# Attention with a fused gated feed-forward: down-projection matmuls cut into smaller pieces, buffers tracked by halves, and the last outputs finished in halves

## The chip, the cores and the metric

The kernel runs on one core of a Trainium2 chip. Five engines work on their own queues: TensorE (PE; its weight loads are shown as PEld), VectorE (DVE), ScalarE (ACT), GpSimd (POOL) and SyncE (SP), which here only issues DMAs. The metric is device time in microseconds of one launch; lower is better.

## The reference

`x` has 2048 rows and 448 columns. The core of the computation is:

```
xn = layernorm(x)
q  = (xn @ wq) as 16 heads of 256;  k, v = last 512 rows of the caches, 8 heads, each used by 2 query heads
s  = softmax(q k^T / 16) v, heads side by side, @ wo            # wo: 4096 x 448
g  = silu((gelu(xn @ w_gate) * (xn @ w_up)) @ w_down)           # 448 -> 1792 -> 448
out = x + s * g
```

The kernel folds `wo` into the values: for each head, V Wo (512 x 448) is computed once, and then P V Wo takes the place of P V and the output projection.

## The kernel before

The whole instruction order is written out by hand. `K.op` records an operation with the buffers that it reads and writes; a planner turns them into semaphore waits. Two records that name the same buffer object are ordered, even if they touch different halves of it. Each engine executes its own operations in the order of recording, so an operation that waits holds up all that is behind it on its engine. Every matmul is recorded by `mms` (L384 in the profile), every ScalarE operation with a plain function by `act` (L378).

**Stage 1** (to about 119 us): layer norm, gate and up projections; V Wo of heads 0 and 1 and the down tiles 0 to 7 (a down tile is 128 rows of `g`, 14 matmuls of 448 columns) are done in it.

**Stage 2, V Wo** (119 to 158 us): the loop over `order`. It alternates half a down tile (7 matmuls, PSUM bank 4 or 5) with `vw_head`: 8 matmuls of one head into four banks of the ring 0, 1, 2, 3, 6, 7. Down tiles 8 to 13 are done here. Heads 13, 14 and 15 come last with nothing between them, and heads 14 and 15 both use banks 0 to 3. `vw_mm` empties a bank: for row blocks 0 and 1 ScalarE writes part 0 (L713) and VectorE part 4 from the bank and part 0 (L715); for blocks 2 and 3 ScalarE writes parts 1 and 2 (L719). `vw_sums` (L726, VectorE) then forms the parts 5, 6 and 3. The seven parts are the right-hand sides of a seven-product (Strassen-Winograd) scheme for P V. Each part holds two row blocks, jj = 0 and 1, and is one buffer `b_vw[h][part]`.

A finished down tile goes through `down_gate`: ScalarE Tanh, VectorE product (L581), and a DMA of the gate to DRAM, issued by `store_g`.

**Stage 3**: the first queries, then 128 steps; step n is head n % 16 of the 256-row chunk n // 16. `halves` issues matmuls on the two 64-row halves of TensorE side by side. In step n TensorE computes the scores of step n (`s_jobs`, two tiles in the banks 4, 5, 6 in rotation), the queries of step n + 2 (`q_jobs`; bank 7, and in the first four steps bank 1 for the second half of the columns), and P V of step m = n - 4 (`pv_plan`, seven products into banks 0 to 3, which add up over the 16 heads of a chunk). VectorE takes the reciprocal of the last step's row sums (`rd`, L863), two row minima (L852) and the four sums of P blocks of step n - 3 (`sums`, L888); ScalarE copies the queries out of PSUM (`q_evac`) and takes two exponentials (`expo`, L857); GpSimd normalises P (L873) and SyncE transposes it with a DMA. The order on VectorE and ScalarE is that of these lines:

```
            row_min(n, 0)
            if more:
                q_evac(n + 2)
            ...
            row_min(n, 1)
            expo(n, 0)
            expo(n, 1)
            if 3 <= n < NST - 1:
                sums(n - 3, (0, 1, 2))
                if ends:
                    evac(1, "dve")
                sums(n - 3, (3,))
```

In the steps 0 to 3 there is no P V. `fill(0)` before the steps and `fill(1)` to `fill(3)` after the steps 0 to 2 do the last two down tiles, 14 and 15, in halves of 7 matmuls.

**Chunk ends.** At steps n = 19, 35, ... 115 (`ends`) a chunk's seven sums are copied out of the banks 0 to 3: `evac(0)` and `evac(1)` on VectorE, `evac(2)` and `evac(3)` on ScalarE. `finish` makes a list of small operations (adds on GpSimd, products with the gate on VectorE), and each following step pops one from `todo`. For most chunks these are 13 operations on 224 columns; for the last chunk but one (c = 6, finished in chunk 7's steps) they are 8 operations on up to 448 columns.

**The end.** The last four heads (P V of steps 124 to 127) are done as plain products after the loop. For this `vw_plain` (L1045, VectorE) forms a further sum for the heads 12 to 15, in the steps 123 to 126, and `gates_scaled` (ScalarE) scales the last two gates, in the steps 120 and 123.

Of the kernel before, what the change touches and what calls it, by code (L numbers as in the profile page):

```python
# [166 lines left out]
def bass_recurrent_scan__sliding_block_cached__geglu_ffn__prompt_kernel(  # L167
# [36 lines left out]
    with es:  # L204
# [80 lines left out]
        vw, a, _ = place("vw", [P, Hq, 7, 2, HN], F16, at=rv)  # L285
        b_vw = [[K.buf(a + vslot(h) * VWB + p * 2 * HN * 2, 2 * HN * 2) for p in range(7)] for h in range(Hq)]
        aS, a, at = place("aS", [P, 7, HN], F32, at=tl)
# [80 lines left out]
        x_view = A_x.rearrange("b (t p) d -> p (b t) d", p=P)  # L368
        out_view = out.rearrange("b (t p) d -> p (b t) d", p=P)

        def dma(q, o, i, reads=(), writes=()):
# [335 lines left out]
        def vw_mm(h, j, i):  # L707
            o, b = bank[i][:, 0:D], b_ps[i]
            mms([(o, vT_at(h // 2)[:, e, j * P:(j + 1) * P], wo_at(2 * h + e), e == 0, e == 1) for e in range(2)],
                [b_vT[h // 2], b_wo[h]], (b,))  # L710
            v, jj = vw[:, vslot(h), :, :, :], j % 2
            if j < 2:
                K.op("act", lambda e: e.activation(v[:, 0, jj, :], o[:, 0:HN], ACT.Copy, scale=sc[:, 0:1]),  # L713
                     (b, b_sc), (b_vw[h][0],))
                K.op("dve", lambda e: e.scalar_tensor_tensor(  # L715
                    out=v[:, 4, jj, :], in0=o[:, HN:D], scalar=sc[:, 0:1], in1=v[:, 0, jj, :],
                    op0=ALU.mult, op1=ALU.subtract), (b, b_sc, b_vw[h][0]), (b_vw[h][4],))
            else:
                K.op("act", lambda e: e.activation(  # L719
                    v[:, 1:3, jj, :], o.rearrange("p (a n) -> p a n", a=2), ACT.Copy, scale=sc[:, 0:1]),  # L720
                    (b, b_sc), b_vw[h][1:3])

        def vw_sums(h):
            v = vw[:, vslot(h), :, :, :]
            for o, a, b in ((5, 2, 4), (6, 5, 0), (3, 1, 5)):
                K.op("dve", lambda e, o=o, a=a, b=b: e.tensor_tensor(v[:, o, :, :], v[:, a, :, :], v[:, b, :, :], ALU.subtract),  # L726
                     (b_vw[h][a], b_vw[h][b]), (b_vw[h][o],))

        def vw_head(h, banks, last=True):
            K.reuse(b_vw[h])  # L730
# [94 lines left out]
        def q_evac(n):  # L825
            s, i = n % NQT, bq(n)
            if 2 <= n < 2 + LAG:
                for e, i in ((0, 7), (1, 1)):
                    act(qT[:, s, e, :], bank[i][:, e * CW:(e + 1) * CW], ACT.Copy, (b_ps[i],), b_qT[s][e:e + 1], scale=NEG)
            else:  # L830
                act(qT[:, s, :, :].rearrange("p e q -> p (e q)"), bank[i], ACT.Copy, (b_ps[i],), b_qT[s], scale=NEG)
# [46 lines left out]
        def sums(n, parts):  # L878
# [7 lines left out]
            for p in parts:  # L886
# [6 lines left out]
                          ((4, 0), (4, 1), (5, 0), (5, 1)), ((3, 0), (3, 1)))  # L893
        FIRST = {(0, (1, 0)), (0, (4, 0)), (0, (3, 0)), (1, (6, 0))}
        LAST = {(1, (2, 1)), (0, (7, 1)), (1, (5, 1)), (1, (3, 1))}
# [8 lines left out]
        def pv_jobs(n, u, lst, last):  # L904
            h, src = n % Hq, pv_src(n)
            rows = slice(R * u, R * u + R)
            out = []
            for p, j in lst:
                i, s = AT[p]
                a, b = src[p]  # L910
                out.append([i, s * HN, (s + 1) * HN, a[rows, j, :], vw[rows, vslot(h), p - 1, j, :],
                            h == 0 and (u, (p, j)) in FIRST, (u, (p, j)) in last, [b, b_vw[h][p - 1]]])
            return out

        def pv_plan(n):
            if n % Hq == Hq - 1:
                one, mid, two, all_ = B0 + B2 + B1[:1], B3, B1[1:], B0 + B1 + B2 + B3
            elif n % Hq == 0:
                one, mid, two, all_ = B0 + B2, (), B3 + B1, B0[:2] + B1 + B0[2:] + B2 + B3
            else:  # L920
                one, mid, two, all_ = B0 + B2, (), B1 + B3, B1 + B3 + B2 + B0
            last = LAST if n % Hq == Hq - 1 else TLAST if n == NST - LAG - 1 else ()
            u = 0 if n + LAG + 2 < NST else 1
            return [pv_jobs(n, u, x, last) for x in (one, mid, two)] + [pv_jobs(n, 1 - u, all_, last)]

        def flat(x):
            return [z for y in x for z in y]

# [27 lines left out]
        def finish(c, eng):  # L956
# [32 lines left out]
            a1, a0, a6 = tt([1], [0], [1]), tt([0], [2], [5]), tt([6], [0], [6])  # L989
            if c == NC - 2:  # L990
                z = (0, 1)
                return [a1, a0, tt([4, 5], [3], [4, 5]), fin(1, z), a6, add(1, z), fin(0, z), add(0, z)]
            u, v = (0,), (1,)
            return [a1, a0, tt([4], [3], [4]), fin(1, u), tt([5], [3], [5]), fin(1, v), add(1, u), fin(0, u), a6,
                    add(1, v), fin(0, v), add(0, u), add(0, v)]

        heads = [*range(3, 13), 2, 13]
        order = []
        for i, h in enumerate(heads):
            order += [8 + i / 2, h]  # L1000
        order += [14, 15]
        ring = [0]

        def banks4():
            r = [(0, 1, 2, 3, 6, 7)[(ring[0] + i) % 6] for i in range(4)]
            ring[0] += 4
            return r

        for k in order:
            if isinstance(k, float):  # L1010
                t, f = int(k), 0 if k == int(k) else NF // 2
                i = 4 + t % 2
                down_mm(t, bank[i][:, 0:D], [b_ps[i]], f, f + NF // 2)
                if f:
                    down_gate(t, bank[i][:, 0:D], [b_ps[i]])
                    store_g()
            elif k < 14:
                vw_head(k, banks4())
                if k in (8, 10):
                    y = k // 10  # L1020
                    K.reuse(b_xq[y])
                    load_xq(y)
            else:
                vw_head(k, (0, 1, 2, 3))
        js = [[q_jobs(n, e) for e in range(2)] for n in range(2)]
# [7 lines left out]

        def fill(k):
            t, i, f = NT - 2 + k // 2, (0, 2)[k // 2], k % 2 * NF // 2
            down_mm(t, bank[i][:, 0:D], [b_ps[i]], f, f + NF // 2)
            if f:
                down_gate(t, bank[i][:, 0:D], [b_ps[i]])
        K.reuse(b_p32 + flat(b_pn) + b_pT[:3] + flat(b_sS[:2]) + b_tmpr + b_g2r)

        VW12 = {NST - LAG - 1 + i: Hq - LAG + i for i in range(LAG)}

        def vw_plain(h):
            v = vw[:, vslot(h), :, :, :]
            K.op("dve", lambda e: e.tensor_tensor(v[:, 6, :, :], v[:, 4, :, :], v[:, 0, :, :], ALU.add),  # L1045
                 (b_vw[h][4], b_vw[h][0]), (b_vw[h][6],))

# [3 lines left out]
        b_gsl = sbuf_bufs(a, D * 4, 2)  # L1051
        GS = {NST - 8: 0, NST - 5: 1}

        def gates_scaled(t):
# [4 lines left out]
        todo, stores, ready = [], [], []  # L1059
        fill(0)  # L1060
        for n in range(NST):
            h, m = n % Hq, n - LAG
            c = n // Hq
            more = n + 2 < NST
            ends = m >= 0 and m % Hq == Hq - 1
            if n == LAG:
                store_g()
                K.reuse(b_pT[3:] + b_sS[2])
            s0, s1 = s_jobs(n, 0, True), s_jobs(n, 1, not more)
            for t in ready:  # L1070
# [4 lines left out]
            if more:  # L1075
                q0, q1 = q_jobs(n + 2, 0), q_jobs(n + 2, 1)
                q0[1][0][5] = True
                (q1[0] if m >= 0 else q1[1])[-1][6] = True
                if m < 0:
                    q1[0][0][5] = q0[0][-1][6] = True  # L1080
            if m < 0:
                halves(q1[0] + s0[0] + q0[0] + s1[0], q0[1] + s1[1] + q1[1] + s0[1])
            else:
# [17 lines left out]
            if 3 <= n < NST - 1:  # L1101
                sums(n - 3, (0, 1, 2))
                if ends:
                    evac(1, "dve")
                sums(n - 3, (3,))
            if n < 3:
                fill(n + 1)
            if n == 2:
                store_g()
            if n in VW12:  # L1110
                vw_plain(VW12[n])
            if n in GS:
                gates_scaled(GS[n])
            if n == LAG:
# [3 lines left out]
            if ends:  # L1118
                evac(3, "act")
                todo.extend(finish(m // Hq, "pool"))  # L1120
            elif todo:
                todo.pop(0)()
            if h == LAG and c >= 1 and c + 1 < NC:
# [51 lines left out]
        for n, t in [(n, t) for n in range(NST - LAG, NST - 2) for t in range(2)] + [  # L1175
# [6 lines left out]
                  n == NST - LAG and j == 0, n == NST - 1 and j == 3) for j in range(4)],  # L1182
                [b_late[t] if n == NST - 1 else b_pT[x]] + [b_vw[h][k] for k in (0, 1, 2, 6)], [b_ps[i]])
        for t in range(2):
# [62 lines left out]
```

## Time and profile before

| | |
|---|---|
| time, median of 3 runs (lowest to highest) | 556.69 us (556.63 to 556.80) |
| the profiled execution's own time | 556.68 us |
| its span, first to last instruction | 554.9 us |
| granted TensorE clock, mean | 1.000 |
| busy: PE, PEld, DVE, ACT, POOL | 98%, 79%, 84%, 62%, 45% of the span |
| stage 2 with the first queries and the first half tile | 119.1 to 161.7 us |
| steps 0 to 4 | 161.7 to 177.2 us |

A line of the timeline gives the start and the length in us, the engine, the line of the kernel, the operation, what it writes and reads, how many instructions were merged, and in brackets how long the engine stood idle before and what ended the wait. A busy TensorE is not TensorE at its best rate: matmuls are pipelined and their ends are modelled, so a small delay can show as a longer distance between starts and not as idle time.

### The profile page before, as it was taken

To read this page: it belongs to the slowest core of one execution; us is meant where nothing else is said; L and a number is where in the kernel's file an instruction comes from. 1 tells how busy PE (TensorE), PEld (TensorE's weight loads), DVE (VectorE), ACT (ScalarE), POOL (GpSimd) and SP (SyncE) were. 2 spreads that over 40 slices of the span, in tenths; PEclk is the share of its full clock that TensorE was granted. 3 is DMA by queue.
4 is the path that set the end of the run, shared out by engine and by line. 5 is a ranking of instruction groups with operands and counts; after the bars stand their busy time and mean duration, and the time that the engine had idled before them with its cause. 6 is when DMAs were issued, how large, how long until landed. Compare 5 with 4: busy or idle time off the path is not lost.

```text
span 554.9 us, 18732 instructions
## 1 busy us (share of the span) xinstructions
PE 544.7 (98%) x7612; PEld 437.6 (79%) x7612; DVE 465.5 (84%) x1196; ACT 341.3 (62%) x813; POOL 250.3 (45%) x385
## 2 busy tenths in 40 slices
PE   8999999999989999999999999999999999999996
PEld 5544444445546999999999999999999999999983
DVE  6674979867757888988988898898989889889996
ACT  5432323477766676776766676676676666666762
POOL 1121590100004444566465465555556555564655
PEclk9999999999999999999999999999999999999999
DMA  9998999401105866566675775576686477566665
GB/s 274 178 242 146 226 270 216 103 1 41 41 8 97 132 108 97 96 98 105 128 107 102 128 108 93 117 125 107 91 135 107 89 128 118 94 108 125 89 106 81
DMA packets 190246, 66.07 MB, mean 119 GB/s; under 512 B 169408, under 2 KB 187984, under 8 KB 190160
## 3 DMA queue, kind: packets, MB, share of 16 engines
q1 hardware_dynamic: 186928, 56.96, 59.6%
q0 software_dynamic: 2464, 7.34, 4.5%
q8 instruction: 60, 0.98, 0.7%
q10 hardware_dynamic: 768, 0.57, 0.3%
q14 instruction: 26, 0.21, 0.2%
HBM read 19.76 MB, written 5.77 MB: 46 GB/s over the span
## 4 chain that ended last, share of the span: by engine, by line
PE 86%; DVE 9%; DMA 2%; issue 1%; ACT 1%; POOL 0%; SPq 0%; DVEq 0%; ACTq 0%
PE bank L384 86%; DVE mn L852 1%; DVE sS L888 1%; DVE vw L715 1%; DVE vw L726 1%; DVE actT L559 1%; DMA x<-in_A_x_dram 1%; DMA pT<-pn 1%; ACT vw L713 1%; DVE mx L676 1%; DVE xn L457 0%; DVE stats L431 0%; ACT gl L378 0%; DVE g2a L581 0%; POOL rstd L443 0%
## 5 line engine op out<-in xcount | busy, mean ns | idle before, releaser
L384 PE MATMUL bank<-kT,qT 64*128 64x512 bf16 x1024 | 279.1, 376 | 0.0
L873 POOL TENSOR_SCALAR pn<-p,rd 128x512 f16<-128x512 f32 x254 | 173.1, 695 | 227.6 <-DVE rd L863 227.6
L384 PE MATMUL bank<-vw,sS 64*128 64x224 f16 x1984 | 222.3, 256 | 0.8 <-DVE sS L888 0.5
L384 PE MATMUL bank<-xq,wq 64*128 64x256 bf16 x1536 | 218.5, 269 | 0.1
L384 PE MATMUL bank<-vw,pT 64*128 64x224 f16 (+1 forms) x1520 | 208.7, 258 | 0.8 <-DMA pT<-pn 0.8
L852 DVE TENSOR_REDUCE mn<-bank 128x1 f32<-128x512 f32 x256 | 173.9, 683 | 35.3 <-PE bank L384 32.5
L857 ACT ACTIVATE p<-bank,mn 128x512 f32<-128x512 f32 x256 | 175.1, 685 | 5.4 <-PE bank L384 3.2
L384 PEld LDWEIGHTS bank<-vw,sS 64*128 64x128 f16 x1984 | 160.7, 94 | 7.8 <-DVE sS L888 2.5
L378 ACT ACTIVATE qT<-bank 128x512 bf16<-128x512 f32 (+1 forms) x132 | 76.6, 584 | 116.6 <-PE bank L384 115.5
L384 PEld LDWEIGHTS bank<-vw,pT 64*128 64x128 f16 (+1 forms) x1520 | 142.5, 94 | 6.1 <-DMA pT<-pn 1.5
L384 PEld LDWEIGHTS bank<-xq,wq 64*128 64x128 bf16 x1536 | 139.6, 94 | 9.4 <-issue 1.9
L384 PEld LDWEIGHTS bank<-kT,qT 64*128 64x128 bf16 x1024 | 93.5, 94 | 2.1 <-ACT p L857 1.2
L888 DVE TENSOR_TENSOR sS<-pT 128x256 f16<-128x256 f16 x248 | 89.8, 402 | 0.0
L384 PE MATMUL bank<-xnT,wgu 64*128 64x512 bf16 (+2 forms) x768 | 84.5, 350 | 0.8 <-DVE actT L559 0.3
L384 PE MATMUL bank<-xq,wqr 64*128 64x256 bf16 x256 | 67.5, 269 | 0.0
L384 PEld LDWEIGHTS bank<-xnT,wgu 64*128 64x128 bf16 x768 | 36.6, 94 | 38.3 <-DVE actT L559 1.1
L378 ACT ACTIVATE gl<-bank 128x512 bf16<-128x512 f32 x56 | 33.1, 597 | 48.5 <-PE bank L384 40.1
L857 ACT ACTIVATION_READ_ACCUMULATOR p<-bank,mn 128x1 f32 x256 | 50.7, 198 | 0.0
L559 DVE TENSOR_TENSOR actT<-bank,gl 128x512 bf16<-128x512 f32 x56 | 37.4, 686 | 15.5 <-PE bank L384 14.8
L384 PE MATMUL bank<-wd,actT 128*128 128x448 bf16 x224 | 45.4, 353 | 0.6 <-DVE actT L559 0.5
L888 DVE TENSOR_TENSOR sS<-pT,sS 128x256 f16<-128x256 f16 x124 | 36.1, 291 | 4.0
L384 PEld LDWEIGHTS bank<-wd,actT 128*128 128x128 bf16 x224 | 21.3, 98 | 22.7 <-issue 1.7
(83 smaller groups left out, 418.5 us busy)
## 6 DMA issues: line engine op xcount, KB each, us to landing
wq<-in_A_wq_dram POOLq DMA_DIRECT2D x8, 384.0 KB, 9.7
woa<-in_A_wo_dram POOLq DMA_DIRECT2D x6, 448.0 KB, 5.3
pT<-pn SPq DMA_TRANSPOSE x129, 3.1
xn_t<-xnT SPq DMA_DIRECT2D x16, 128.0 KB, 3.6
xr<-in_A_x_dram SPq DMA_DIRECT2D x16, 112.0 KB, 2.6
gr<-gate_t SPq DMA_DIRECT2D x16, 112.0 KB, 2.7
out_dram<-ofin SPq DMA_DIRECT2D x16, 112.0 KB, 2.0
wd<-in_B_w_down_dram SPq DMA_DIRECT2D x1, 1568.0 KB, 8.1
```

The costliest lines, as they stand in the source:

```text
L378: K.op("act", lambda e, o=o, i=i: e.activation(o, i, func, scale=scale), reads, writes)
L384: ins = e.matmul(o, lhsT=l, rhs=r, start=st, stop=sp)
L559: K.op("dve", lambda e: e.tensor_tensor(actT[c % 2][:, f, :], bank[b + 1], gl[:, s, :], ALU.mult), (b_ps[b + 1], b_gl[s]), (b_actT[c % 2][ ...
L676: K.op("dve", lambda e: e.tensor_reduce(mx[:, i:i + 1], o, AX.XY, ALU.max, apply_absolute_value=True), (b,), (b_mx,))
L713: K.op("act", lambda e: e.activation(v[:, 0, jj, :], o[:, 0:HN], ACT.Copy, scale=sc[:, 0:1]), (b, b_sc), (b_vw[h][0],))
L715: K.op("dve", lambda e: e.scalar_tensor_tensor(out=v[:, 4, jj, :], in0=o[:, HN:D], scalar=sc[:, 0:1], in1=v[:, 0, jj, :], op0=ALU.mult, op ...
L726: K.op("dve", lambda e, o=o, a=a, b=b: e.tensor_tensor(v[:, o, :, :], v[:, a, :, :], v[:, b, :, :], ALU.subtract), (b_vw[h][a], b_vw[h][b] ...
L852: K.op("dve", lambda e: e.tensor_reduce(mn[:, m:m + 1], bank[i], AX.X, ALU.min), (b_ps[i],), (b_mn[m],))
L857: K.op("act", lambda e: e.activation(p32[:, z, :], bank[i], ACT.Exp, bias=mn[:, m:m + 1], scale=-1.0, accum_out=rsum[:, 2 * r + t:2 * r + ...
L873: K.op(engs[t], lambda e, o=o, i=i, s=s: e.tensor_scalar(o, i, s, 1.0, op0=ALU.mult, op1=ALU.mult), (b_p32[z], b_rd[r]), (b_pn[y][t],))
L888: o = K.op("dve", lambda e, i=i, a=a, b=b, f=f: e.tensor_tensor(s[i], a, b, f), r, (b_sS[y][i],))
```

## The change

Seven things are changed.

1. `b_vw` has a buffer for each half (jj = 0, 1) of each part. Every user of it names the halves it touches.
2. The down tiles 8 to 15 (112 matmuls) are cut into 19 pieces by `down_piece(n)`, which goes on where the last piece ended, across tiles: 6 or 7 matmuls before each of the first twelve heads, 6 before head 14, 4 before head 15, 4 before the first step, and 5 after each of the steps 0 to 3. Tile 14 uses bank 0 as before, tile 15 bank 3 (bank 2 before). Head 14 uses the banks 1, 2, 3, 6, and head 15 7, 1, 2, 3.
3. In the first four steps the second half of the queries is copied out of bank 1 by VectorE, between the two row minima; the first half stays on ScalarE. The matmuls of these steps begin with the scores in one half and with the queries in the other.
4. At a chunk end `evac(1)` stands after the first two sums, not after the first three, and the first P V of a chunk takes part 7 before part 6 in bank 1.
5. The first finishing operation is popped in the chunk-end step itself.
6. The last chunk but one is finished in 13 small operations like the others; at steps 120 and 124 two are popped.
7. `vw_plain` of the heads 12 and 13 moves from the steps 123 and 124 to 113 and 114, and both `gates_scaled` to step 126.

The diff, cut to its core:

```diff
-        b_vw = [[K.buf(a + vslot(h) * VWB + p * 2 * HN * 2, 2 * HN * 2) for p in range(7)] for h in range(Hq)]
+        b_vw = [[sbuf_bufs(a + vslot(h) * VWB + p * 2 * HN * 2, HN * 2, 2) for p in range(7)] for h in range(Hq)]
...
                 K.op("act", lambda e: e.activation(v[:, 0, jj, :], o[:, 0:HN], ACT.Copy, scale=sc[:, 0:1]),
-                     (b, b_sc), (b_vw[h][0],))
+                     (b, b_sc), (b_vw[h][0][jj],))
...
-                for e, i in ((0, 7), (1, 1)):
-                    act(qT[:, s, e, :], bank[i][:, e * CW:(e + 1) * CW], ACT.Copy, (b_ps[i],), b_qT[s][e:e + 1], scale=NEG)
+                act(qT[:, s, 0, :], bank[7][:, 0:CW], ACT.Copy, (b_ps[7],), b_qT[s][0:1], scale=NEG)
+                K.op("dve", lambda e: e.tensor_scalar(qT[:, s, 1, :], bank[1][:, CW:2 * CW], NEG, None, op0=ALU.mult),
+                     (b_ps[1],), b_qT[s][1:2])
...
-        FIRST = {(0, (1, 0)), (0, (4, 0)), (0, (3, 0)), (1, (6, 0))}
+        FIRST = {(0, (1, 0)), (0, (4, 0)), (0, (3, 0)), (1, (7, 0))}
...
-                one, mid, two, all_ = B0 + B2, (), B3 + B1, B0[:2] + B1 + B0[2:] + B2 + B3
+                one, mid, two, all_ = B0 + B2, (), B3 + B1, B0[:2] + B1[2:] + B1[:2] + B0[2:] + B2 + B3
...
-            if c == NC - 2:
-                z = (0, 1)
-                return [a1, a0, tt([4, 5], [3], [4, 5]), fin(1, z), a6, add(1, z), fin(0, z), add(0, z)]
...
+        down_at = [NT // 2 * NF]
+        def down_piece(n):
+            while n:
+                t, f = divmod(down_at[0], NF)
+                k = min(n, NF - f)
+                i = 4 + t % 2 if t < NT - 2 else (0, 3)[t - NT + 2]
+                down_mm(t, bank[i][:, 0:D], [b_ps[i]], f, f + k)
+                down_at[0] += k
+                n -= k
+                if f + k == NF:
+                    down_gate(t, bank[i][:, 0:D], [b_ps[i]])
+                    if t < NT - 2:
+                        store_g()
         heads = [*range(3, 13), 2, 13]
+        ring = (0, 1, 2, 3, 6, 7)
         for i, h in enumerate(heads):
-            order += [8 + i / 2, h]
-        order += [14, 15]
+            down_piece(6 + (i in (0, 3, 5, 8, 10, 11)))
+            vw_head(h, [ring[(4 * i + j) % 6] for j in range(4)])
...
+        down_piece(6)
+        vw_head(14, (1, 2, 3, 6))
+        down_piece(4)
+        vw_head(15, (7, 1, 2, 3))
...
-        VW12 = {NST - LAG - 1 + i: Hq - LAG + i for i in range(LAG)}
+        VW12 = {NST - Hq + 1: 12, NST - Hq + 2: 13, NST - 3: 14, NST - 2: 15}
...
-        GS = {NST - 8: 0, NST - 5: 1}
...
-        fill(0)
+        down_piece(4)
         for n in range(NST):
...
-                halves(q1[0] + s0[0] + q0[0] + s1[0], q0[1] + s1[1] + q1[1] + s0[1])
+                halves(s0[0] + s1[0] + q0[0] + q1[0], q0[1] + q1[1] + s0[1] + s1[1])
...
-                sums(n - 3, (0, 1, 2))
+                sums(n - 3, (0, 1))
                 if ends:
                     evac(1, "dve")
-                sums(n - 3, (3,))
-            if n < 3:
-                fill(n + 1)
+                sums(n - 3, (2, 3))
+            if n < LAG:
+                down_piece(5)
...
-            if n in GS:
-                gates_scaled(GS[n])
+            if n == NST - 2:
+                gates_scaled(0)
+                gates_scaled(1)
...
                 todo.extend(finish(m // Hq, "pool"))
-            elif todo:
-                todo.pop(0)()
+            for _ in range(2 if n - NST + Hq in (8, 12) else 1):
+                if todo:
+                    todo.pop(0)()
```

More of the change, by code (lines that the diff above doesn't have):

```diff
@@ L369, in bass_recurrent_scan__sliding_block_cached__geglu_ffn__prompt_kernel, with flat @@
         out_view = out.rearrange("b (t p) d -> p (b t) d", p=P)
+        def flat(x):
+            return [z for y in x for z in y]
         def dma(q, o, i, reads=(), writes=()):
@@ L713, in vw_mm @@
                 K.op("act", lambda e: e.activation(v[:, 0, jj, :], o[:, 0:HN], ACT.Copy, scale=sc[:, 0:1]),
-                     (b, b_sc), (b_vw[h][0],))
+                     (b, b_sc), (b_vw[h][0][jj],))
                 K.op("dve", lambda e: e.scalar_tensor_tensor(
                     out=v[:, 4, jj, :], in0=o[:, HN:D], scalar=sc[:, 0:1], in1=v[:, 0, jj, :],
-                    op0=ALU.mult, op1=ALU.subtract), (b, b_sc, b_vw[h][0]), (b_vw[h][4],))
+                    op0=ALU.mult, op1=ALU.subtract), (b, b_sc, b_vw[h][0][jj]), (b_vw[h][4][jj],))
             else:
@@ L720, in vw_mm @@
                     v[:, 1:3, jj, :], o.rearrange("p (a n) -> p a n", a=2), ACT.Copy, scale=sc[:, 0:1]),
-                    (b, b_sc), b_vw[h][1:3])
+                    (b, b_sc), (b_vw[h][1][jj], b_vw[h][2][jj]))
         def vw_sums(h):
@@ L726, in vw_sums @@
                 K.op("dve", lambda e, o=o, a=a, b=b: e.tensor_tensor(v[:, o, :, :], v[:, a, :, :], v[:, b, :, :], ALU.subtract),
-                     (b_vw[h][a], b_vw[h][b]), (b_vw[h][o],))
+                     b_vw[h][a] + b_vw[h][b], b_vw[h][o])
         def vw_head(h, banks, last=True):
-            K.reuse(b_vw[h])
+            K.reuse(flat(b_vw[h]))
             for j, i in zip((0, 2, 1, 3), banks):
@@ L911, in pv_jobs @@
                 out.append([i, s * HN, (s + 1) * HN, a[rows, j, :], vw[rows, vslot(h), p - 1, j, :],
-                            h == 0 and (u, (p, j)) in FIRST, (u, (p, j)) in last, [b, b_vw[h][p - 1]]])
+                            h == 0 and (u, (p, j)) in FIRST, (u, (p, j)) in last, [b, b_vw[h][p - 1][j]]])
             return out
@@ L924, in pv_plan @@
             return [pv_jobs(n, u, x, last) for x in (one, mid, two)] + [pv_jobs(n, 1 - u, all_, last)]
-        def flat(x):
-            return [z for y in x for z in y]
         def load_xq(c):
@@ L995, in finish @@
                     add(1, v), fin(0, v), add(0, u), add(0, v)]
+        down_at = [NT // 2 * NF]
[11 more added lines that the diff above has]
+                        store_g()
         heads = [*range(3, 13), 2, 13]
-        order = []
+        ring = (0, 1, 2, 3, 6, 7)
         for i, h in enumerate(heads):
-            order += [8 + i / 2, h]
-        order += [14, 15]
[L1002 to L1024, printed above, removed]
+            down_piece(6 + (i in (0, 3, 5, 8, 10, 11)))
+            vw_head(h, [ring[(4 * i + j) % 6] for j in range(4)])
+            if h in (8, 10):
+                y = h // 10
+                K.reuse(b_xq[y])
+                load_xq(y)
+        down_piece(6)
+        vw_head(14, (1, 2, 3, 6))
+        down_piece(4)
+        vw_head(15, (7, 1, 2, 3))
         js = [[q_jobs(n, e) for e in range(2)] for n in range(2)]
@@ L1032, in bass_recurrent_scan__sliding_block_cached__geglu_ffn__prompt_kernel @@
             q_evac(n)
[L1034 to L1038, printed above, removed]
         K.reuse(b_p32 + flat(b_pn) + b_pT[:3] + flat(b_sS[:2]) + b_tmpr + b_g2r)
-        VW12 = {NST - LAG - 1 + i: Hq - LAG + i for i in range(LAG)}
+        VW12 = {NST - Hq + 1: 12, NST - Hq + 2: 13, NST - 3: 14, NST - 2: 15}
         def vw_plain(h):
@@ L1045, in vw_plain @@
             K.op("dve", lambda e: e.tensor_tensor(v[:, 6, :, :], v[:, 4, :, :], v[:, 0, :, :], ALU.add),
-                 (b_vw[h][4], b_vw[h][0]), (b_vw[h][6],))
+                 b_vw[h][4] + b_vw[h][0], b_vw[h][6])
         ends_at = ((NT - 2) % NXR, (NT - 1) % NXR)
@@ L1065, in bass_recurrent_scan__sliding_block_cached__geglu_ffn__prompt_kernel @@
             ends = m >= 0 and m % Hq == Hq - 1
+            if n in (2, LAG):
+                store_g()
             if n == LAG:
-                store_g()
                 K.reuse(b_pT[3:] + b_sS[2])
-            s0, s1 = s_jobs(n, 0, True), s_jobs(n, 1, not more)
+            s0, s1 = s_jobs(n, 0, True), s_jobs(n, 1, not more or m < 0)
             for t in ready:
@@ L1076, in bass_recurrent_scan__sliding_block_cached__geglu_ffn__prompt_kernel @@
                 q0, q1 = q_jobs(n + 2, 0), q_jobs(n + 2, 1)
-                q0[1][0][5] = True
-                (q1[0] if m >= 0 else q1[1])[-1][6] = True
+                q0[1][0][5] = q1[0][-1][6] = True
                 if m < 0:
-                    q1[0][0][5] = q0[0][-1][6] = True
+                    q1[1][0][5] = q0[0][-1][6] = True
             if m < 0:
-                halves(q1[0] + s0[0] + q0[0] + s1[0], q0[1] + s1[1] + q1[1] + s0[1])
+                halves(s0[0] + s1[0] + q0[0] + q1[0], q0[1] + q1[1] + s0[1] + s1[1])
             else:
@@ L1101, in bass_recurrent_scan__sliding_block_cached__geglu_ffn__prompt_kernel @@
             if 3 <= n < NST - 1:
-                sums(n - 3, (0, 1, 2))
+                sums(n - 3, (0, 1))
                 if ends:
                     evac(1, "dve")
-                sums(n - 3, (3,))
-            if n < 3:
-                fill(n + 1)
-            if n == 2:
-                store_g()
+                sums(n - 3, (2, 3))
+            if n < LAG:
+                down_piece(5)
             if n in VW12:
                 vw_plain(VW12[n])
-            if n in GS:
-                gates_scaled(GS[n])
+            if n == NST - 2:
+                gates_scaled(0)
+                gates_scaled(1)
             if n == LAG:
@@ L1182, in bass_recurrent_scan__sliding_block_cached__geglu_ffn__prompt_kernel @@
                   n == NST - LAG and j == 0, n == NST - 1 and j == 3) for j in range(4)],
-                [b_late[t] if n == NST - 1 else b_pT[x]] + [b_vw[h][k] for k in (0, 1, 2, 6)], [b_ps[i]])
+                [b_late[t] if n == NST - 1 else b_pT[x]] + [b_vw[h][k][z] for k in (0, 1, 2, 6) for z in range(2)], [b_ps[i]])
         for t in range(2):
```

## The prediction

> **What bounds the kernel now.** I read the page first: busy shares and the chain that ended last.
>
> ```profile
> PE 544.7 (98%) x7612; PEld 437.6 (79%) x7612; DVE 465.5 (84%) x1196; ACT 341.3 (62%) x813; POOL 250.3 (45%) x385
> ...
> PE 86%; DVE 9%; DMA 2%; issue 1%; ACT 1%; POOL 0%; SPq 0%; DVEq 0%; ACTq 0%
> ```
>
> TensorE sets the time; the change keeps its arithmetic, so it can win only where TensorE stands still or moves slowly, and VectorE holds 9% of the chain. So I went through the timeline for the places. From 119.11 on, TensorE alternates seven down matmuls with eight V Wo matmuls without a gap, 15 in 2.85 us (0.19 each). At the end of the stage this breaks:
>
> ```profile
> 150.33 1.49 PE L384 MATMUL bank<-wd,actT 128*128 128x448 bf16 x7
> 151.66 3.19 PE L384 MATMUL bank<-woa,vTa 128*128 128x448 bf16 x16
> 156.50 1.99 PE L384 MATMUL bank<-woa,vTa 128*128 128x448 bf16 x8 [1.65 <-DVE vw L715]
> 158.42 0.83 PE L384 MATMUL bank<-xq,wq 64*128 64x256 bf16 x12
> ```
>
> Heads 13, 14, 15 follow each other with no down piece between, and 14 and 15 use the same four banks; TensorE waits 1.65 us for VectorE to empty one. The same timeline, all engines, shows the first steps (first line: a half down tile of step 0) and the first P V step, where VectorE's sums come late:
>
> ```profile
> 163.46 1.50 PE L384 MATMUL bank<-wd,actT 128*128 128x448 bf16 x7
> ...
> 165.70 0.54 ACT L378 ACTIVATE tmpr<-bank 128x448 f32<-128x448 f32 x1
> ...
> 166.34 0.62 DVE L581 SCALAR_TENSOR_TENSOR g2r<-tmpr,bank 128x448 bf16<-128x448 f32 x1 [1.49 <-PE bank L384]
> ...
> 175.25 0.27 PE L384 MATMUL bank<-vw,sS 64*128 64x224 f16 x1 [0.55 <-DVE sS L888]
> ```
>
> Last, I took the first score matmul of each step (every eighth bank<-kT,qT matmul). Steps are 2.97 us apart, except: steps 0 to 4 (161.72 to 177.22, 15.50 us); 3.09 once after each of the seven chunk ends; and 3.26, 3.17 and 3.27 at steps 119, 122, 124, all in the tail, where VectorE never waits between merged pieces:
>
> ```profile
> 530.45 0.68 DVE L973 SCALAR_TENSOR_TENSOR tmp<-aS,sc,gr 128x448 f32<-128x448 f32 x1
> 531.05 0.15 DVE L863 RECIPROCAL rd<-rsum 128x2 f32<-128x2 f32 x1
> ...
> 534.29 0.39 DVE L1045 TENSOR_TENSOR vw<-vw 128x448 f16<-128x448 f16 x1
> 534.59 0.16 DVE L863 RECIPROCAL rd<-rsum 128x2 f32<-128x2 f32 x1
> ```
>
> One rd line is one VectorE step: this one took 3.54.
>
> **Part 1, V Wo stage.** Before: 119.11 to the start of step 0 at 161.72 is 42.61 us, with 91 down and 112 V Wo matmuls (203 x 0.19 = 38.6) and 1.87 for the first queries. After: 92 down. Pieces of 6 and 4 now stand between the last heads. One head's evacuation runs 1.84 on ScalarE (issue to issue 0.35 + 0.51 + 0.35 + 0.63) and 1.86 on VectorE (0.74 + 1.12), less than the new 14 x 0.19 = 2.66 per head; the gate, 0.54 and 0.62 once per 14 down matmuls, adds 0.27 a head and still fits. Separate halves remove ScalarE's waits for VectorE (6.9 us over the run), which made a head cost 2.57 at the end. Walking heads 13 to 15 with these durations: head 14 needs bank 2 at 3.04 us after head 13 starts (free at 1.4), head 15 bank 1 at 5.32 (free 4.6) and bank 3 at 6.1 (free 5.1); only the query matmuls wait for bank 7, 0.2 us. Sum: 204 x 0.19 = 38.76, queries 1.87 (their gaps are those of two halves that share banks), waits 0.2: step 0 starts at 159.95. **Gain 1.77.** Bounds: no wait 2.0; one more bank wait like the old 1.65 gives 0.3.
>
> **Part 2, steps 0 to 4.** Alone, a step's halves take 1.74 (161.72 to 163.46), seven down matmuls 1.42, so a piece costs 0.09 beyond 0.19 each (the change from half-row to full matmuls and back; five pieces for four). After: 1.74 + 5 x 0.19 + 0.09 = 2.78, four times 11.12; pieces no longer stop before step 3, so 0.95 us of matmuls cover the sums that TensorE waited for.
> The new cost is on VectorE. The copy of half a query, 128x256 from PSUM, isn't in the trace; the nearest rows are the 128x224 PSUM add (0.39) and the 128x448 copy (0.62). I take 0.38 issue to issue, ends 0.3 and 0.6. It sits between the two row minima: reciprocal 0.08, minimum 0.60, copy 0.38, minimum 0.69, exponential 0.78, two hand-overs 0.14, then the next reciprocal: 2.67, within 2.78. But tile 14's gate now falls into step 1, behind its exponentials: Tanh 0.54 and product 0.62 delay step 2's first minimum by 0.9, its exponential ends at 9.4 us after step 0's start, and step 3's second score tile wants that bank at 8.8. I book 0.65 of stall in step 3. Step 4 starts at 11.8, its sums are ready (12.4 for the first, wanted at 12.8), it takes 2.97, and 0.1 stays for VectorE's lag. Sum 11.12 + 0.65 + 2.97 + 0.1 = 14.84 against 15.50: **gain 0.66**, bounds 1.4 (no stall: 4 x 2.78 + 2.97 = 14.09) and -0.4 (each of the two gates stalls by 0.8 and a copy of 0.6 lengthens the loop past the step).
>
> **Part 3, seven chunk ends.** The bank-1 evacuation moves one operation earlier:
>
> ```profile
> 222.68 0.28 DVE L888 TENSOR_TENSOR sS<-sS,pT 128x256 f16<-128x256 f16 x1
> 222.88 0.81 DVE L950 TENSOR_TENSOR aS<-bank,aS 128x224 f32<-128x224 f32 x2
> 223.61 0.28 DVE L888 TENSOR_TENSOR sS<-pT,sS 128x256 f16<-128x256 f16 x1
> 223.81 0.16 DVE L863 RECIPROCAL rd<-rsum 128x2 f32<-128x2 f32 x1
> ```
>
> Now the last two sums stand side by side, and the second reads the first: in other steps such a pair is spaced 0.31 (219.43, 219.74) instead of 0.20, so everything behind, the next reciprocal first, comes 0.12 later. In the next step the third sum was in time by only 0.03 (needed 1.635 into the step, there at 1.60), so TensorE pays about 0.09 each. GpSimd's first finishing add moves into the same step and runs 221.7 to 222.4 beside a row minimum; I cost it at nothing because the minimum is still running (222.37) when it ends, and beside the sums it costs about 0.4 (Part 4). The 3.09 itself comes from ScalarE (a score tile waiting for an exponential, 0.18 idle at 223.07), which stays. **Loss 0.6**, bounds 0 and 0.9 with that cover.
>
> **Part 4, last chunk.** Small pieces on GpSimd beside VectorE, in an earlier chunk:
>
> ```profile
> 242.83 0.61 POOL L984 TENSOR_TENSOR ofin<-tmp,xr 128x224 bf16<-128x224 f32 x1
> ```
>
> ```profile
> 242.93 0.86 DVE L888 TENSOR_TENSOR sS<-pT 128x256 f16<-128x256 f16 x2
> ...
> 245.90 0.48 DVE L888 TENSOR_TENSOR sS<-pT 128x256 f16<-128x256 f16 x2
> ```
>
> VectorE's sums wait until GpSimd is through: 0.38 for one small add. While VectorE is behind, a step with one small piece takes 2.87 there, without any 2.40 (2.70 less 0.30 for V Wo), with merged pieces 3.0 to 3.38. VectorE's steps 115 to 125 take 33.98 now (506.02 to 540.00). After: 3.81 + 0.13 for the chunk end, seven single steps at 2.87, two double steps at 2.40 + 0.47 + 0.43 = 3.30, step 125 with an add and a V Wo sum 2.40 + 0.47 + 0.30 = 3.17: 33.80. **Gain 0.2**: splitting gives back nearly all that spreading wins. Bounds: 1.0 if VectorE keeps up (TensorE's extra 0.29 + 0.20 + 0.30 gone and 0.2 of lag), -0.6 if doubles collide worse.
> Split products alone: 2 x 0.36 issue to issue against 0.60 for the whole one (530.45 to 531.05), 0.12 dearer a pair, two pairs; this is inside the 2.87 and 3.30.
> [...]
> At nothing: the V Wo sums of heads 12 and 13 in steps 113 and 114 (VectorE idles 0.48 there for TensorE, a sum takes 0.30; else 0.3 each); both gate scalings on ScalarE in step 126 (issued 0.58 apart, 1.24 in all; ScalarE idles 1.25 before the last exponentials, so at worst 0.1); tile 12's store, now behind the last transpose on SyncE (that transpose lands 0.6 before use; else up to 1.3, the spread of transposes in this trace).
>
> **Sum.** 1.77 + 0.66 - 0.6 + 0.2 = 2.0 us. The profiled execution took 556.68, the median is 556.69: 554.7.
>
> **Rivals.** (a) Slower. The early GpSimd add falls on the sums and not on the minimum. Then each chunk end costs 0.12 + 0.47 = 0.59, 4.1 in all, and the other parts' gains of 2.6 are overrun: 558.2. It decides from 0.53 per end, where the time passes 557.8. For it: VectorE there has no idle time for a step on; against: the row minimum covers the add to within 0.1. 0.10. (b) The waits only change place: step 3's stall repeats in step 4, head 15 waits for a bank, gains shrink to 1.3 and chunk ends take 0.9: 556.3, no measurable change (0.2% is 1.1 us, about what a measurement of this kernel can tell from none). 0.18. (c) All cover holds: 2.0 + 1.4 + 1.0 and no loss at the ends: 552.3. For it: VectorE waits for row minima through most steps, against it the dependence of the two sums. 0.20. My forecast, 553.6 to 555.5, has 0.52.
>
> **How the numbers follow.** Faster is forecast plus (c), 0.72; same (b), 0.18; slower (a), 0.10. The range leaves (a) out and half of the far side of (c): 552.8 to 556.6.
>
> **What would show it.** Right: no TensorE gap over 0.5 between V Wo heads, step 0 starting near 160.0 and step 5 near 174.8; a wait of some 0.6 for ScalarE or VectorE in step 3; the step after each chunk end still 3.09 and the one behind it 3.05 instead of 2.97; in the last chunk 2.87 for VectorE's steps with one piece and 3.3 for the two doubles. Wrong: step 5 later than 176, chunk ends growing by over 0.3, or the reciprocal of step 125 moved by more than 1 us against TensorE's step 116.

## The result and the profile after

The changed kernel takes 555.0 us, median of 7 runs (554.54 to 555.64), beside 556.69 (556.36 to 557.84, 7 runs) for the kernel before: 1.69 us less, ratio 0.9967, 95% interval 0.9955 to 0.9978. It is faster, by about as much as was forecast (554.7). The profiled execution took 554.54, the lowest of the seven; its span is 552.7 against 554.9.

The page of the profile after, busy time and the chain that ended last:

```profile
PE 545.0 (99%) x7612; PEld 437.2 (79%) x7612; DVE 464.7 (84%) x1202; ACT 339.8 (61%) x809; POOL 249.8 (45%) x388
...
PE 91%; DVE 5%; DMA 2%; issue 1%; ACT 1%; POOL 0%; SPq 0%; DVEq 0%; ACTq 0%
```

The work is the same; VectorE's share of the chain fell from 9% to 5% and TensorE's rose by the same. The timeline of TensorE at the end of the V Wo stage:

```profile
152.03 1.30 PE L387 MATMUL bank<-wd,actT 128*128 128x448 bf16 x6
153.17 1.68 PE L387 MATMUL bank<-woa,vTa 128*128 128x448 bf16 x8
154.68 0.92 PE L387 MATMUL bank<-wd,actT 128*128 128x448 bf16 x4
155.44 1.68 PE L387 MATMUL bank<-woa,vTa 128*128 128x448 bf16 x8
157.05 1.04 PE L387 MATMUL bank<-xq,wq 64*128 64x256 bf16 x12
```

No bracket is left, so there is no recorded wait between the heads; the 12 query matmuls take 1.04 and not 0.83, about the 0.2 that was forecast for bank 7, though the profile names no wait there. Step 0 starts at 160.00. VectorE in the steps 1 and 2, and TensorE's weight loads in step 3:

```profile
165.13 0.68 DVE L856 TENSOR_REDUCE mn<-bank 128x1 f32<-128x512 f32 x1
167.22 0.62 DVE L584 SCALAR_TENSOR_TENSOR g2r<-tmpr,bank 128x448 bf16<-128x448 f32 x1 [1.42 <-ACT tmpr L381]
167.76 0.16 DVE L867 RECIPROCAL rd<-rsum 128x2 f32<-128x2 f32 x1
167.84 0.67 DVE L856 TENSOR_REDUCE mn<-bank 128x1 f32<-128x512 f32 x1
168.42 0.41 DVE L832 TENSOR_SCALAR qT<-bank 128x256 bf16<-128x256 f32 x1
```

```profile
169.37 0.09 PEld L387 LDWEIGHTS bank<-kT,qT 64*128 64x128 bf16 x1 [0.32 <-ACT p L861]
```

The gate product of tile 14 waits 1.42 us for its Tanh and holds back step 2's minima; TensorE then waits for the exponential. Step 3 takes 3.37 us where steps 0, 1 and 2 take 2.79. VectorE at a chunk end:

```profile
220.22 0.81 DVE L951 TENSOR_TENSOR aS<-bank,aS 128x224 f32<-128x224 f32 x2
220.94 0.28 DVE L892 TENSOR_TENSOR sS<-sS,pT 128x256 f16<-128x256 f16 x1
221.26 0.29 DVE L892 TENSOR_TENSOR sS<-pT,sS 128x256 f16<-128x256 f16 x1
221.47 0.15 DVE L867 RECIPROCAL rd<-rsum 128x2 f32<-128x2 f32 x1
```

The last two sums are 0.32 apart and the reciprocal comes 3.93 after the one before (3.81 before the change). And a double step in the last chunk, 519.72 to 523.06, with a small add on GpSimd (521.29, 0.61 us) beside its sums and a product behind them:

```profile
521.29 0.61 POOL L985 TENSOR_TENSOR ofin<-tmp,xr 128x224 bf16<-128x224 f32 x1
```

```profile
521.34 0.91 DVE L892 TENSOR_TENSOR sS<-pT 128x256 f16<-128x256 f16 x2
...
522.70 0.45 DVE L974 SCALAR_TENSOR_TENSOR tmp<-aS,sc,gr 128x224 f32<-128x224 f32 x1
523.06 0.16 DVE L867 RECIPROCAL rd<-rsum 128x2 f32<-128x2 f32 x1
```

Profiles start stage 2 at different times (118.6 to 120.7), which hides differences of half a microsecond. These arise in the first 60 us: from the 401st gate and up matmul (57.0 to 59.1) to the start of stage 2 every trace takes 61.62 to 61.65. So the kernels are compared by distances inside one profile: from the first down matmul of stage 2 to step 0 (A), from step 0 to step 5 (B), the length of the step behind a chunk end's first one (C), from the first down matmul to the reciprocal of step 125 (D, which sums A, B, the chunk ends and the last chunk), and from the reciprocal of step 126 to the end (E). Step 0 starts here with its first matmul, the other steps with their first score matmul. There is one trace of each kernel, so A to E are of one execution, and the times of several.

| kernel | A | B | C | D | E | time, us | ratio to before (95%) |
|---|---|---|---|---|---|---|---|
| before | 42.61 | 15.51 | 2.97 | 420.89 | 12.20 | 556.69 | |
| changed | 40.89 | 14.70 | 3.10 | 418.94 | 11.99 | 555.0 | 0.9967 (0.9955 to 0.9978) |
| e1_order | 40.88 | 14.72 | 2.97 | 418.27 | 12.80 | 554.66 | 0.9966 (0.9954 to 0.9978) |
| e2_pop | 40.89 | 14.71 | 3.10 | 419.06 | 12.12 | 554.85 | 0.9967 (0.9954 to 0.9979) |
| e3_whole | 42.70 | 14.71 | 3.11 | 420.92 | 12.19 | 556.73 | 1.0006 (0.9997 to 1.0014) |
| e4_qact | 40.89 | 14.50 | 3.11 | 418.83 | 13.06 | 555.26 | 0.9973 (0.9964 to 0.9981) |
| e5_front | 40.88 | 14.72 | 2.97 | 418.39 | 12.83 | 555.38 | 0.9967 (0.9955 to 0.9980) |
| e6_defer | 40.88 | 14.13 | 3.11 | 418.42 | 13.05 | 555.3 | 0.9965 (0.9953 to 0.9977) |
| e7_both | 40.89 | 14.12 | 2.97 | 417.62 | 12.76 | 554.23 | 0.9946 (0.9932 to 0.9960) |
| e9_halves | 41.58 | 15.51 | 2.97 | 419.91 | 12.11 | 556.33 | 0.9973 (0.9964 to 0.9983) |
| e10_pad10 | 40.89 | 14.12 | 2.97 | 417.65 | 12.07 | 553.59 | 0.9944 (0.9932 to 0.9957) |
| e12_pad3 | 40.88 | 14.13 | 2.97 | 417.61 | 13.01 | 555.11 | 0.9964 (0.9951 to 0.9978) |
| e11_before_pad13 | 42.61 | 15.50 | 2.97 | 420.88 | 12.02 | 556.97 | 0.9998 (0.9983 to 1.0013) |

The kernel before took 556.58 beside e1 to e4, 557.4 beside e5, e6, e7 and e9, and 556.83 beside the last three, so times of different groups go by their ratios.

### The profile page after: what moved, and what is told of

Read it like the earlier page. It is cut to its first block, busy times and chain, and to the rows that moved or that the text cites. A ratio compares the mean times of both kernels' runs of the same rounds, so it can differ in the third digit from the quotient of the medians.

```text
span 552.7 us, 18715 instructions
## 1 busy us (share of the span) xinstructions
PE 545.0 (99%) x7612; PEld 437.2 (79%) x7612; DVE 464.7 (84%) x1202; ACT 339.8 (61%) x809; POOL 249.8 (45%) x388
## 4 chain that ended last, share of the span: by engine, by line
PE 91%; DVE 5%; DMA 2%; issue 1%; ACT 1%; POOL 0%; SPq 0%; DVEq 0%; ACTq 0%
PE bank L387 91%; DVE mn L856 1%; DVE actT L562 1%; DMA x<-in_A_x_dram 1%; DMA pT<-pn 1%; DVE mx L679 1%; DVE sS L892 1%; DVE xn L460 0%; DVE stats L434 0%; ACT gl L381 0%; POOL rstd L446 0%; SPq L375 0%; ACT p L861 0%; DVE qT L832 0%; DVE p L1121 0%
## 5 line engine op out<-in xcount | busy, mean ns | idle before, releaser
L387 PE MATMUL bank<-xq,wq 64*128 64x256 bf16 x1536 | 221.9, 269 | 0.1
L387 PEld LDWEIGHTS bank<-vw,sS 64*128 64x128 f16 x1984 | 164.1, 94 | 7.9 <-DVE sS L892 2.5
L387 PEld LDWEIGHTS bank<-xq,wq 64*128 64x128 bf16 x1536 | 141.7, 94 | 10.0 <-PE bank L387 0.7
L387 PEld LDWEIGHTS bank<-kT,qT 64*128 64x128 bf16 x1024 | 95.1, 94 | 4.1 <-ACT p L861 1.5
L892 DVE TENSOR_TENSOR sS<-pT 128x256 f16<-128x256 f16 x248 | 86.3, 388 | 0.0
```

The lines of the kernel that those rows point to most:

```text
L387: ins = e.matmul(o, lhsT=l, rhs=r, start=st, stop=sp)
L892: o = K.op("dve", lambda e, i=i, a=a, b=b, f=f: e.tensor_tensor(s[i], a, b, f), r, (b_sS[y][i],))
```

## The experiments

**The V Wo stage: pieces without halves (e3_whole).**

```diff
-        b_vw = [[sbuf_bufs(a + vslot(h) * VWB + p * 2 * HN * 2, HN * 2, 2) for p in range(7)] for h in range(Hq)]
+        b_vw = [[[K.buf(a + vslot(h) * VWB + p * 2 * HN * 2, 2 * HN * 2)] * 2 for p in range(7)] for h in range(Hq)]
```

> The changed kernel with one buffer for both halves of each V Wo part, as in the kernel before; pieces, banks and all else stay. Theory: the halves are needed because the pieces are shorter. Without them a head's evacuation takes 2.57 and with the gate's 0.27 a head 2.84, against 2.66 of matmuls; TensorE loses up to 0.18 a head once the ring's lead of about one head is used up, and the last heads wait again: step 0 starts between 160.5 and 162 instead of 160.0, time 555.5 to 557. Rival, the pieces between the last heads do it all: step 0 at 160.0, 555.0 us.

A is 42.70: the pieces and the new banks alone win nothing (the kernel before has 42.61, and the time is the old one, 1.0006). TensorE's timeline of e3_whole at the end of the stage:

```profile
155.50 0.54 PE L387 MATMUL bank<-woa,vTa 128*128 128x448 bf16 x2
156.41 1.62 PE L387 MATMUL bank<-woa,vTa 128*128 128x448 bf16 x6 [0.37 <-DVE vw L718]
157.96 0.28 PE L387 MATMUL bank<-xq,wq 64*128 64x256 bf16 x1
158.99 0.82 PE L387 MATMUL bank<-xq,wq 64*128 64x256 bf16 x11 [0.75 <-DVE vw L718]
```

The waits only moved, into head 15 and behind it: evacuation is slower than the shorter pieces, as expected. The waits of the stage show the reason for the halves (what waits, for what, us in total, times, longest). The kernel before, then e3_whole, then the changed kernel, each with ScalarE's longest wait before writing a part:

```profile
ACT vw L713 <- DVE vw L715: 6.0, 13, 0.8
```

```profile
ACT vw L716 <- DVE vw L718: 8.7, 12, 0.9
```

```profile
ACT vw L716 <- PE bank L387: 6.7, 11, 1.0
```

With whole buffers ScalarE waits for VectorE; in the changed kernel, and in e9_halves below, no such wait is recorded, and it waits for TensorE.

**Halves without pieces (e9_halves):** the kernel before, with item 1 alone.

> The kernel before with only the V Wo halves tracked apart; pieces, banks and all else as before. Theory: a head's evacuation falls from 2.57 to about 1.86, so the wait before head 15 falls from 1.65 to about 1.0 and the short one inside it goes; step 0 starts at about 160.7 instead of 161.72 after the same beginning, time 555.7. With e3_whole (pieces without halves: no gain) that would make the two needed together. Rival: the halves alone bring all of it, step 0 at 160.0, time 554.9.

A is 41.58, 1.03 less. In its timeline head 15 waits less:

```profile
156.56 1.69 PE L384 MATMUL bank<-woa,vTa 128*128 128x448 bf16 x8 [0.93 <-DVE vw L715]
```

0.93 in place of 1.65, and the eight matmuls take 1.69 in place of 1.99. So halves alone bring 1.03, pieces alone nothing, both together 1.72. The pieces and the new banks of heads 14 and 15 were not tried apart, so what each has in the other 0.69 is open.

**The chunk ends (e1_order, e2_pop).** e1_order restores the old order of `evac(1)`, `FIRST` and `all_`; e2_pop undoes the early pop before the last chunk:

```diff
-                sums(n - 3, (0, 1))
+                sums(n - 3, (0, 1, 2))
                 if ends:
                     evac(1, "dve")
-                sums(n - 3, (2, 3))
+                sums(n - 3, (3,))
```

```diff
-            for _ in range(2 if n - NST + Hq in (8, 12) else 1):
+            for _ in range(2 if n - NST + Hq in (8, 12) else 0 if ends and n < NST - Hq else 1):
```

> The changed kernel with the chunk-end order of the kernel before: evac(1) after three sums, part 6 before part 7 in bank 1. The early pop and all else stay. Theory: the two sums that now stand side by side make VectorE's chunk-end step 3.93 us instead of 3.81, and TensorE pays for it one step later. So VectorE's step goes back to 3.81, TensorE's steps behind a chunk end go from 3.07 and 3.10 back to 3.09 and 2.97, and the time falls by 7 x 0.11 = 0.8 us, to about 554.2. Rival, the early GpSimd add is the cause: 3.10 stays, the time stays at 555.0.

> The changed kernel without the early pop at the six chunk ends before the last: the first finishing add runs one step later, as in the kernel before. The new order of sums and evac(1) stays. Theory: no effect, VectorE's chunk-end step stays 3.93 and TensorE's next-but-one step 3.10; 555.0 us. Rival, the early GpSimd add is the cause: 3.10 becomes 2.97 at six chunk ends, 0.8 us less, 554.2.

The same four operations in e1_order:

```profile
220.18 0.28 DVE L892 TENSOR_TENSOR sS<-sS,pT 128x256 f16<-128x256 f16 x1
220.38 0.81 DVE L951 TENSOR_TENSOR aS<-bank,aS 128x224 f32<-128x224 f32 x2
221.11 0.28 DVE L892 TENSOR_TENSOR sS<-pT,sS 128x256 f16<-128x256 f16 x1
221.31 0.16 DVE L867 RECIPROCAL rd<-rsum 128x2 f32<-128x2 f32 x1
```

In e1_order VectorE's chunk-end step is 3.81 again, TensorE's two steps 3.09 and 2.97, and D falls by 0.67: the order is the cause. The P V order in bank 1 was put back in the same run; the 0.12 of VectorE's step lies between its own last two sums (0.32 apart in the changed kernel; in e1_order what follows the third comes 0.20 behind it) and can't come from there. In e2_pop 3.93 and 3.10 stay: the early add is innocent. But the time of e1_order fell only by 0.3, and its ratio to before stayed at 0.9966, because E grew by 0.81, of which below.

**The first steps (e4_qact, e6_defer).** e4_qact gives the second query copy back to ScalarE; e6_defer records tile 14's product in step 2:

```diff
+            if t == NT - 2:
+                late_gate.append(product)
+            else:
+                product()
...
             row_min(n, 1)
+            if n == 2:
+                late_gate.pop()()
```

> The changed kernel with both halves of the first queries copied by ScalarE, as before; all else stays. Theory: the copy between the row minima (0.33 from issue to issue) lengthens VectorE's loop, and the loop together with tile 14's gate makes the 0.58 us stall of step 3. Without the copy step 2's first minimum starts 0.3 earlier, step 3 falls from 3.37 to about 3.1, time 0.2 to 0.3 less, 554.75. Rival, ScalarE needs the relief: a second copy of 0.38 in front of each exponential delays them, and the steps 0 to 3 get longer by 0.1 to 0.3 each, time 555.3 or more.

> The changed kernel with VectorE's product of tile 14's gate recorded in step 2, behind its second row minimum, not in step 1; the Tanh stays. Both late gate stores go out at step 4. Theory: the product, waiting for the Tanh, holds up the row minima of step 2 and so makes the 0.58 stall of step 3. Step 3 falls from 3.37 to 2.79, step 5 starts 0.6 earlier after step 0, time about 554.4. Rival, the bank that VectorE copies queries from or ScalarE's Tanh makes it: 3.37 falls by less than 0.2, 555.0.

In e4_qact step 3 takes 3.16, the steps before it stay at 2.78 and 2.79, and B falls by 0.20: the copy on VectorE costs time here, and ScalarE does not need the relief. In e6_defer the wait of step 3 is gone, all four steps take 2.79 and B falls by 0.57. VectorE of e6_defer, steps 1 and 2:

```profile
167.29 0.69 DVE L864 TENSOR_REDUCE mn<-bank 128x1 f32<-128x512 f32 x1
167.90 0.41 DVE L840 TENSOR_SCALAR qT<-bank 128x256 bf16<-128x256 f32 x1
168.23 0.68 DVE L864 TENSOR_REDUCE mn<-bank 128x1 f32<-128x512 f32 x1
168.83 0.61 DVE L588 SCALAR_TENSOR_TENSOR g2r<-tmpr,bank 128x448 bf16<-128x448 f32 x1
```

The product starts without a bracket: its Tanh was done, and step 2's minima stand in front of it. Neither time shows the gain (e4_qact's 555.26 is near what its rival said, for another reason); in both E is about 13.05.

**The last chunk (e5_front):** items 4 to 7 undone.

> The changed kernel with the chunk ends and the last chunk as before: old order of evac(1), no early pop, finishing in 8 merged operations, V Wo sums in steps 123 to 126, gate scalings in 120 and 123. Only the V Wo stage and the first steps stay changed. Theory: they bring the whole gain, step 5 starts 2.5 earlier than in the kernel before; the last chunk shows 3.26, 3.17, 3.27 again, and the reciprocal of step 125 comes at about 537.5, 0.2 later than in e1_order (537.33): the new finishing is worth 0.2. Time 554.2 to 554.9. Rival, the new finishing is worth the 0.79 that TensorE no longer loses: reciprocal at 538.1, time 555.2 or more.

TensorE's 3.25, 3.17 and 3.26 are back, and D is 418.39 against 418.27 of e1_order. That is a gain of 0.12 from items 6 and 7, near the scatter of single traces. D without A and B, the part that the chunk ends and the last chunk share, says it with more traces: 362.77 to 362.82 with both as before (before, e5_front, e9_halves, e11_before_pad13), 362.60 to 362.67 with the new last chunk alone (e1_order, e7_both, e10_pad10, e12_pad3), 363.35 to 363.51 with both new (changed, e2_pop, e3_whole, e4_qact, e6_defer; they differ in A, B and the early add alone). By the means the last chunk wins 0.16 and the order at the chunk ends costs 0.80. Of what TensorE no longer loses at the steps 119 to 124 it loses most elsewhere: the step behind the last chunk end is 0.08 longer, and one step before the end takes 2.95 to 2.97 in place of 2.44, with waits for VectorE. The time of e5_front, 555.38, lies over the range expected; the kernel before beside it was slower as well, and the ratio, 0.9967, is that of the changed kernel.

**Both repairs (e7_both), and the end (e10_pad10, e12_pad3, e11_before_pad13).**

> e1_order and e6_defer together: the old chunk-end order and the late gate product, the rest as in the changed kernel. Theory: 0.58 and 7 x 0.11 add up, the reciprocal of step 125 comes 1.3 earlier than in the changed kernel (538.05), at about 536.75; the time falls by 0.4 to 1.3 to 553.7 to 554.6, where the spread comes from how long the last four transposes of P take. Rival: what is won in front is waited for at the end, 555.0.

D fell by 1.32, as the parts add up, and 554.23 is in the range expected. (The trace is of an execution of 555.07, in which stage 2 starts late, at 120.16; four of the six took 553.96 to 554.27.) E is 12.76, and the table has only two kinds of E: 11.99 to 12.20 and 12.76 to 13.06. The trace's DMA records have one thing that goes with it. Instructions are fetched by DMAs, of 16 KB (queue q8) and 8 KB (q14); the page of the profile after has

```profile
q8 instruction: 60, 0.98, 0.8%
q14 instruction: 26, 0.21, 0.1%
```

A 16 KB fetch begins within 0.7 us of the reciprocal of step 126 in all thirteen traces. Where E is long, an 8 KB fetch begins 4.6 to 5.3 us behind the reciprocal of step 126, among the last transposes of P; where E is short, it comes earlier (by 1.5 us or more before that reciprocal) or after the transposes (10.7). VectorE has 8 records less in e7_both than in the changed kernel. In the changed kernel's trace eight of q14's fetches, from 180.93 to 539.24 us, stand 127 to 131 VectorE records apart (its waits counted; the fetch's record names no engine), so padding might move it:

```diff
+        for k in range(10):        # 3 in e12_pad3; 13, in the kernel before, in e11_before_pad13
+            K.op("dve", lambda e, k=k: e.memset(pad[:, k:k + 1], 0.0))
```

> e7_both with ten one-column memsets more on VectorE, put where it idles 2.2 us before the first step. Why: in five of ten traces an 8 KB fetch of instructions starts between 545.0 and 546.9, while the last transposes of P are in flight, and from the reciprocal of step 126 to the end these take 12.8 to 13.1; in the other five, with that fetch elsewhere, 12.0 to 12.2. VectorE's own count of instructions decides where the fetch falls (it has 8 records less in e7_both than in the changed kernel). Theory: the fetch moves to about 540, the end takes 12.1 instead of 12.76, time 0.6 less than e7_both, about 553.6 and a ratio of 0.9935 or less to the kernel before. Rival: the transposes' times scatter for other reasons, end 12.8, ratio 0.9946 as for e7_both.

> e7_both with three memsets more in the same place, against e10_pad10: the memsets are the same kind, the fetch moves less. Theory: it falls at about 543.5 to 544.5, still among the last transposes, end 12.6 or more from the reciprocal of step 126, time as e7_both. Rival, memsets as such shorten the end: as e10_pad10.

> The kernel before with thirteen one-column memsets more on VectorE in its idle time before the first step. There the 8 KB fetch is at 553.4, behind the last transposes, and the end takes 12.2. Theory: the fetch moves forward to about 545, into the last transposes, and the end grows to about 12.9; all steps stay as in the kernel before; time 0.7 more than the kernel before. Rival: no change, 12.2.

In e10_pad10 the fetch went to 535.68, further than the 540 expected, E is 12.07, the steps are those of e7_both, and the time 553.59; the ratio, 0.9944, is not the 0.9935 expected. In e12_pad3 it did not move (5.25 behind the reciprocal), E is 13.01. The third missed its aim: the fetch went to 541.39, before the last four transposes, and E stayed short, 12.02, which fits the rule but does not test it. Weight loads at the end, e7_both and then e10_pad10:

```profile
543.57 1.25 PEld L387 LDWEIGHTS bank<-vw,pT 128*128 128x128 f16 x8 [0.88 <-DMA pT<-pn]
545.45 0.49 PEld L387 LDWEIGHTS bank<-vw,pT 128*128 128x128 f16 x4 [0.64 <-DMA pT<-pn]
546.90 2.01 PEld L387 LDWEIGHTS bank<-vw,pT 128*128 128x128 f16 x12 [0.96 <-DMA pT<-pn]
```

```profile
542.89 1.25 PEld L387 LDWEIGHTS bank<-vw,pT 128*128 128x128 f16 x8 [1.00 <-DMA pT<-pn]
544.65 2.76 PEld L387 LDWEIGHTS bank<-vw,pT 128*128 128x128 f16 x16 [0.52 <-DMA pT<-pn]
```

The third wait is gone. It was for the first transpose of step 127, which lands 3.36 us after its issue in e7_both, 3.63 in e12_pad3 and 2.50 in e10_pad10. e10_pad10 has the lowest median here: 3.2 us less than the kernel before beside it, ratio 0.9944. Beside e12_pad3, in the same group, it is 1.5 faster; of the 1.45 between their spans, E has 0.94 and the start of stage 2 0.54. Whether it also beats e7_both by the 0.6 seen in the medians isn't settled by the ratios (0.9944 and 0.9946).

## Why the prediction was right

**Part 1.** Step 0 was forecast at 159.95 and came at 160.00 (stage 2 starts at 119.11 in both profiles), and the only delay left is the 0.2 before the queries. The prediction's ground for it was that separate halves end ScalarE's waits for VectorE and so bring evacuation under 2.66 a head. e3_whole and e9_halves show both: without halves ScalarE's waits stay and nothing is won, with halves they are gone.

**Part 2.** B was forecast as 14.84 and is 14.70. (Both count from the first query matmul of step 0, in the kernel before at 161.72; the first score matmul, which the prediction names, is at 162.06 there.) The stall of step 3 was 0.58, forecast 0.65, and e6_defer shows that its cause is the one named, the gate product of tile 14 in front of step 2's minima. The copy, put at 0.38 from issue to issue, measured 0.33; e4_qact shows that it adds 0.20 to that stall. The 0.1 kept for VectorE's lag in step 4 was not needed: it takes 2.98.

**Part 3.** Forecast 0.09 an end, measured 0.11 (3.07 and 3.10 against 3.09 and 2.97), 0.77 in seven, where 0.6 was booked. Reason and place are shown by e1_order, and the cost of the early add, put at nothing, by e2_pop. Rival (a) rested on that add falling on the sums; it does not.

**Part 4.** VectorE's steps 115 to 125 were forecast at 33.80; they took 33.63. The miss is all in step 115 (3.75, forecast 3.94); the other ten took 29.88, forecast 29.86, with singles of 2.76 to 3.02 and doubles of 3.34 for 2.87 and 3.30. The net gain by D is 1.95 - 1.72 - 0.81 + 0.77 = 0.19, and 0.16 by the means above, forecast 0.2. One thing put at nothing was not quite: the V Wo sum in step 113 lengthens VectorE's step to 3.23, and the step behind the last chunk end takes 3.18 and not 3.10.
A split product still stands 0.36 ahead of what follows it in the profile after (522.70 to 523.06); twice that against the whole one's 0.60 before (530.45 to 531.05) is 0.12 a pair, the price taken from the rows of before.

**The sum.** Forecast 2.0; 2.14 in the profiled executions, 1.69 in the medians. Of the 2.14, D brings 1.95 and the end 0.21, within rounding. That the sum came so near is in part luck: part 2 won 0.14 more than forecast, part 3 lost 0.2 more, and the profiled execution has the shortest end of all traces here. What the prediction did not see is the end: it treated slow transposes as a scatter, and e1_order, e4_qact and e6_defer each lost there what they had won in front.

## What to carry to other kernels

Smaller pieces of one engine's work helped here only with a shorter evacuation behind them (A is 42.70 in e3_whole, without the halves, and 40.89 with them), so shorten that first (here by tracking halves), and then cut. An operation that waits for another engine belongs behind the work of its own queue that others wait for: a 0.62 us product in the wrong place cost 0.58. When a gain shows in the steps and not in the time, compare by distances inside the profile, and look at the last transfers.

## What the runs showed of the hardware

Instruction fetches of 8 KB (0.31 to 1.47 us each over the traces of before and after) go with an end that is 0.8 us longer when they fall among the last DMA transposes: E was 12.76 to 13.06 in the six traces with one there and 11.99 to 12.20 in the seven without. Two kernels that differ only in how many memsets stand in an idle stretch point the same way, with one trace each: e10_pad10, with its fetch moved away, and e12_pad3, with its fetch in the same place. The rest of the run agrees. Of the first 125 transposes of all thirteen traces, the 637 with no instruction fetch in flight between issue and landing took 3.01 to 3.37 us; the 988 with one, of 8 or of 16 KB, took 3.00 to 5.82. So a fetch need not slow a transpose, but none over 3.37 us was without a fetch. Whether and how such a fetch holds a transpose up was not measured, nor what sets the fetch's place exactly: three memsets did not move it, ten moved it by 9 us.
